# First ten MLP steps in plain float32, weights converted a whole tile at a time: a retention layer and two MLPs on one core

## The chip, the core and the metric

One core of a Trainium2 chip runs the whole program. Its engines are TensorE (PE in the profile; PEld is its weight load), VectorE (DVE), ScalarE (ACT), GpSimd (POOL) and SyncE (SP), whose queue issues most transfers (DMA). The metric is the device time of one execution in microseconds; lower is better.

## What is computed

```python
# retention: q, k, v of shape (4, 8, 768, 64)
gamma = 1.0 - 2.0 ** (-5.0 - np.arange(H, dtype=np.float32))
for t in range(S):
    state = gamma * state + np.einsum('bhd,bhe->bhde', k[:, :, t], v[:, :, t])
    y[:, :, t] = scale * np.einsum('bhd,bhde->bhe', q[:, :, t], state)
x = y.transpose(0, 2, 1, 3).reshape(3072, 512)
# MLP 1: 512 -> 2048 -> 512
h = x @ moe_w_in;  x = np.maximum(0.01 * h, h) @ moe_w_out
# MLP 2
h = np.maximum(x @ moe2_w_in, 0.0);  out = (h * h) @ moe2_w_out
```

The weights arrive as 64-bit floats, so the kernel turns them into 32-bit ones.

## The kernel before

**Retention** is done in chunks of 256 positions. A *unit* is one chunk of one batch element (12 units), a *pair* is two heads of one unit (48 pairs). A pair needs scaled q and v on VectorE (`qs`, `vs`, L121 and L122), scores on TensorE (`sc`, L168 and L169 in the first four units, L176 later), a masked product on VectorE (`pm`, L186), a value product on TensorE (`y`, L228 or L208), an outer product for the state (`sp` or `first_acc`, L243) and a copy into `xs`. The buffers of scores, outer products and MLP products come from one pool of three (`ps_h`).

**The MLPs** run in steps. A step takes one tile `j` of 128 of the 2048 hidden columns, for 512 tokens: an input group on TensorE (`emit_in`, product `h`), the activation on ScalarE and VectorE (`activate`, `g`), and an output group (`emit_out`) that adds into `acc`. In reduced precision each operand is split into a rounded value and the rest (`wih`/`wil`, `woh`/`wol`, `xh`/`xl`, `gh`/`gl`: a cast on ScalarE and a subtraction on VectorE), and three products stand for one: 12 of 512 columns in each group. The first `HS` = 5 steps are different: only unit 0 (256 tokens) is ready, and they run in plain float32, four products a group and no splits (L390, L437). Steps 5 to 15 take 512 tokens, steps 16 to 20 the other 256 of the first five tiles; after these 21 steps come blocks of 16, six blocks in each layer. Step `HS` writes its output in two cuts of 256 columns (`widens`).

**Weights.** Tile `j` of a layer is 1 MB in two halves (input and output weights). `load_half` brings one half into a staging buffer (`sg`), `convert` turns it into float32 (`w`): two ScalarE operations on the high and low words (L317, L318), then on VectorE a shift (L319), a merge of the sign (L320) and an add (L323). In the first layer two of three tiles stage in slots that later hold activations and the third in `stage_p`; in the second layer three half-tile buffers take turns.

**Order.** The code is written in step order, but a scheduler sets, when the program is built, the order in which each engine and queue gets its instructions; conversions are pulled ahead of steps where it finds room. On the chip each engine keeps that order, and an instruction that waits holds all behind it.

Of the kernel before, what the change touches and what calls it, by code (L numbers as in the profile page):

```python
# [9 lines left out]
F32 = mybir.dt.float32  # L10
# [19 lines left out]
LEAK = 0.01  # L30
WHOLE = 4
HS = 5
LEAD = 6
AHEAD = 2
AHEAD2 = 4
# [7 lines left out]
def retention_then_two_mlps(  # L43
# [11 lines left out]
    nc = tc.nc  # L55
    const = ctx.enter_context(tc.tile_pool(name="const", bufs=1))
    big_p = ctx.enter_context(tc.tile_pool(name="big", bufs=1))
    stage_p = ctx.enter_context(tc.tile_pool(name="stage", bufs=2))
    wsp_p = ctx.enter_context(tc.tile_pool(name="wsp", bufs=2))
    g_p = ctx.enter_context(tc.tile_pool(name="g", bufs=2))  # L60
    a_p = ctx.enter_context(tc.tile_pool(name="a", bufs=2))
# [11 lines left out]
    def slot(n, shape, dt, name):  # L73
        return big_p.tile(shape, dt, tag=f"x{n}", name=name)
# [87 lines left out]
    def scores(hu):  # L162
        u, p, h = hu
        if u < WHOLE:
            qs, k, vs = prep[u, p]
            a = slice(64 * h, 64 * h + 64)
            sc = ps_h.tile([P, 512], F32, tag="h", name="sc")
            nc.tensor.matmul(out=sc[:, 128:256], lhsT=k[a, P:2 * P], rhs=qs[a, P:2 * P], start=True, stop=True)  # L168
            nc.tensor.matmul(out=sc[:, 256:512], lhsT=k[a, 0:P], rhs=qs[a], start=True, stop=True)  # L169
        else:  # L170
            q2, kh, kl, v2, vs, w2 = prep[u, p]
            sc = ps_h.tile([P, 512], F32, tag="h", name="sc")
            for sb in (1, 0):
                o, c = (P, P) if sb else (C, 0)
                for n, kk in enumerate((kh, kl)):
                    nc.tensor.matmul(  # L176
                        out=sc[:, o:o + C - c], lhsT=kk[:, h * C + sb * P:h * C + (sb + 1) * P], rhs=q2[h][:, c:C],
                        start=n == 0, stop=n == 1,
                    )
        sc_ps[hu] = sc  # L180

# [91 lines left out]


    wraw, stage = {}, {}
    halves = [(lay, j, half) for lay in range(2) for j in range(NJ) for half in range(2)]
    n_loaded, n_conv = [0], [0]
    early_stage = [None]

    def load_half():  # L280
        m = n_loaded[0]
        if m < len(halves):
            lay, j, half = halves[m]
            if lay == 0 and half == 0 and j % 3 < 2:
                early_stage[0] = slot(4 + j % 3, [P, 2, DM], U64, "sg")
            if lay == 0 and j % 3 < 2:
                t = early_stage[0][:, half]
            elif lay == 0:
                t = stage_p.tile([P, DM], U64, tag="sg", name="sg")
            elif m % 3 == 2:  # L290
                t = a_p.tile([P, DM], U64, tag="r", name="sg", bufs=1)
            else:
                t = stage_p.tile([P, DM], U64, tag="sg", name="sg")
            stage[m] = t
            nc.sync.dma_start(out=t, in_=w[lay, j, half])
            n_loaded[0] += 1

    def convert():

        m = n_conv[0]
        n_conv[0] += 1
        lay, j, half = halves[m]
        if half == 0:  # L310
            wraw[lay, j] = rawslot((lay * NJ + j) % NRAW, [P, 2 * DM], F32, "w")
        r = wraw[lay, j][:, half * DM:(half + 1) * DM]
        src = stage.pop(m).bitcast(U32)
        word = src.rearrange("p (n t) -> p n t", t=2)
        lo, hi = word[:, :, 0], word[:, :, 1]
        ru = r.bitcast(U32)
        nc.scalar.activation(out=r, in_=hi.bitcast(F32), func=AF.Copy, scale=2.0 ** -112)  # L317
        nc.scalar.activation(out=lo, in_=lo, func=AF.Copy, scale=2.0 ** -29)  # L318
        nc.vector.tensor_scalar(out=ru, in0=ru, scalar1=3, scalar2=None, op0=ALU.logical_shift_left)  # L319
        nc.vector.scalar_tensor_tensor(  # L320
            out=ru, in0=hi, scalar=0x80000000, in1=ru, op0=ALU.bitwise_and, op1=ALU.bitwise_or,
        )
        nc.vector.tensor_tensor(out=ru, in0=ru, in1=lo, op=ALU.add)  # L323
        if n_loaded[0] < 2 * NJ or lay == 1:
            load_half()
        if m == 0:
            load_half()

    def converted_to(n):
        while n_conv[0] < min(n, len(halves)):  # L330
            convert()


# [18 lines left out]

    def split_w(i, half):
        n, j = steps[i][:2]
        if i < HS:
            (win, wout)[half][i] = wraw[lbs[n][0], j][:, half * DM:(half + 1) * DM]
            return
        src = wraw[lbs[n][0], j][:, half * DM:(half + 1) * DM]
        tag = ("wi", "wo")[half]
        hi = wsp_p.tile([P, DM], F32R, tag=tag + "h", name=tag + "h")  # L360
        lo = wsp_p.tile([P, DM], F32R, tag=tag + "l", name=tag + "l")
        nc.scalar.copy(hi, src)  # L362
        nc.vector.tensor_tensor(out=lo, in0=src, in1=hi.bitcast(F32), op=ALU.subtract)  # L363
        (win, wout)[half][i] = (hi, lo)
# [18 lines left out]
    def emit_in(i):  # L383
        n, j, c0, c1 = steps[i]
        hp = ps_h.tile([P, T], F32, tag="h", name="h")
        h_ps[i] = hp
        if i < HS:
            w, x = win.pop(i), xslot[0]
            for kb in range(KB):
                nc.tensor.matmul(  # L390
                    out=hp[:, :c1 - c0], lhsT=w[:, kb * P:(kb + 1) * P], rhs=x[:, kb, c0:c1],
                    start=kb == 0, stop=kb == KB - 1,
                )
            return
        x = xhl[n]
        wh, wl = win.pop(i)
        for kb in range(KB):
            xh, xl = x[kb]
            for k, (a, b) in enumerate(((wh, xh), (wl, xh), (wh, xl))):
                nc.tensor.matmul(  # L400
                    out=hp[:, :c1 - c0], lhsT=a[:, kb * P:(kb + 1) * P], rhs=b[:, c0:c1],
                    start=kb == 0 and k == 0, stop=kb == KB - 1 and k == 2,
                )

    def activate(i):
        n, j, c0, c1 = steps[i]
        lay, m = lbs[n][0], c1 - c0
        hp = h_ps.pop(i)
        g = g_p.tile([P, T], F32, tag="g", name="g", bufs=1)
        if i >= HS:  # L410
            gh = g_p.tile([P, T], F32R, tag="gh", name="gh")
            gl = g_p.tile([P, T], F32R, tag="gl", name="gl")
        if lay == 0:
            nc.scalar.activation(out=g[:, :m], in_=hp[:, :m], func=AF.Copy, scale=LEAK)  # L414
            nc.vector.tensor_tensor(out=g[:, :m], in0=g[:, :m], in1=hp[:, :m], op=ALU.max)  # L415
        else:
            nc.scalar.activation(out=g[:, :m], in_=hp[:, :m], func=AF.Relu)  # L417
            nc.vector.scalar_tensor_tensor(  # L418
                out=g[:, :m], in0=hp[:, :m], scalar=0.0, in1=g[:, :m], op0=ALU.max, op1=ALU.mult
            )  # L420
        if i < HS:
            gs[i] = g
            return
        nc.scalar.copy(gh[:, :m], g[:, :m])  # L424
        nc.vector.tensor_tensor(out=gl[:, :m], in0=g[:, :m], in1=gh[:, :m].bitcast(F32), op=ALU.subtract)  # L425
        gs[i] = (gh, gl)

    def emit_out(i):
# [2 lines left out]
        if i == first_step[n]:  # L431
            acc[n] = ps_acc.tile([P, 4, T], F32, tag="acc", name="acc")
        ac = acc[n]
        if i < HS:
            g, w = gs.pop(i), wout.pop(i)
            for m in range(4):
                nc.tensor.matmul(  # L437
                    out=ac[:, m, c0:c1], lhsT=w[:, m * P:(m + 1) * P], rhs=g[:, :c1 - c0], start=i == 0, stop=False
                )
            return  # L440
        gh, gl = gs.pop(i)
        wh, wl = wout.pop(i)

        start, stop = i == first_step[n], i == last_step[n]
        cols = [(c0, c1)]
        if i in widens:
            cols = [(c, c + C) for c in range(c0, c1, C)]
        passes = ((wh, gh), (wl, gh), (wh, gl))
        if stop:
            mm = [(k, m) for m in range(4) for k in range(3)]  # L450
# [53 lines left out]

    def need_x(i):
        n, j, c0, c1 = steps[i]
        if i < HS:
            return
        miss = [c for c in range(c0 // C, c1 // C) if (n, c) not in done_x]
        if miss:  # L510
# [20 lines left out]
    nc.scalar.dma_start(out=mk, in_=mask)  # L531
    loads_to(1)
    nc.scalar.dma_start(out=qt[:, 1:4], in_=qtab[:, 1:4])
    loads_to(4)
    for _ in range(5):
        load_half()
    first_acc = ps_acc.tile([P, 4, T], F32, tag="acc", name="first_acc")
    for k in range(NP):
        preps_to(k + 1)
# [5 lines left out]
    split_w(0, 0)  # L545
    emit_in(0)
    activate(0)
    converted_to(2)
    split_w(0, 1)
    converted_to(3)  # L550
    split_w(1, 0)
    converted_to(6)

    for i in range(N):
        n, j, c0, c1 = steps[i]
# [24 lines left out]
            preps_to(ups.index(head_at[i + 1][-1][:2]) + 1)  # L580
            loads_to(n_prep[0] + 1)
        if i < NJ:
            converted_to(min(2 * (i + 1 + AHEAD) + 1, 2 * NJ))
        if i == conv2 - AHEAD2 - 1:
            for _ in range(3):
                load_half()
        elif i >= conv2 - AHEAD2:
            j = i - conv2
            due = 2 * (i + 1 + AHEAD - first_step[NB]) + 1
            converted_to(2 * NJ + max(min(j + AHEAD2, 2 * max(j, 0) + 2), due))  # L590


_OUT = ((NT, DM), "float32")
# [58 lines left out]
```

## Time and profile before

| what | value |
|---|---|
| time, median of 3 runs | 1216.43 us (1216.36 to 1216.61) |
| profiled execution: its time | 1216.53 us |
| profiled execution: span of the trace | 1214.5 us |
| TensorE busy | 1187.4 us (98%) |
| VectorE busy | 863.0 us (71%) |
| ScalarE busy | 691.8 us (57%) |
| moved by DMA | 68.81 MB |

The span runs from the first instruction to the last; about 2 us of the time lie around it. Busy time of TensorE counts matmuls whose ends are modelled, and neighbours overlap, so the distance between the starts of two matmuls says more than their durations. The shares are means over stages that differ: the early stage (retention's first pairs, the first layer's conversions), the long middle, the second layer's conversions around 590 to 700 us, and the second layer.

### The profile page before, as it was taken

Reading aid. Unit: us, or ns where it says so; the run is one execution under the profiler, and the core shown is the slowest. Engines: PE = TensorE matmul, PEld = TensorE weight load, DVE = VectorE, ACT = ScalarE, POOL = GpSimd, SP = SyncE. Lnnn points to the kernel's source line nnn. Section 1 sums busy time; section 2 is a strip of 40 time slices with the busy share of each in tenths; the row PEclk is TensorE's granted clock in tenths of the full one; section 3 lists DMA queues with packets and bytes.
Section 4 is the critical chain, followed back from the end, with each engine's and each line's share of the span. In section 5 each row is a group of like instructions: output and inputs, shape, how many; then the busy total and the mean of one; then the engine's idle time right before and its main releaser. Section 6 shows DMA issues by size and latency. Waiting matters only on the chain.

```text
span 1214.5 us, 15223 instructions
## 1 busy us (share of the span) xinstructions
PE 1187.4 (98%) x5660; PEld 977.7 (81%) x5660; DVE 863.0 (71%) x1621; ACT 691.8 (57%) x1382; POOL 0.2 (0%) x4
## 2 busy tenths in 40 slices
PE   6889999999999999999999999999999999999998
PEld 4667788888888888888888788888888888888886
DVE  6996598889888888978799945644645545545553
ACT  5674476667666766766677644444444444444443
POOL 0000000000000000000000000000000000000000
PEclk9899999999999999999999999999999999999999
DMA  9662111111111111111145300000000000000000
GB/s 343 238 232 86 45 51 45 44 44 49 61 40 36 40 48 35 35 53 48 40 157 179 99 1 1 35 1 1 35 1 1 36 1 1 35 1 1 35 1 35
DMA packets 22825, 68.81 MB, mean 57 GB/s; under 512 B 2784, under 2 KB 5088, under 8 KB 22752
## 3 DMA queue, kind: packets, MB, share of 16 engines
q1 hardware_dynamic: 22032, 67.12, 16.3%
q8 instruction: 44, 0.72, 0.2%
q10 hardware_dynamic: 720, 0.73, 0.2%
q14 instruction: 29, 0.24, 0.1%
HBM read 61.55 MB, written 6.29 MB: 56 GB/s over the span
## 4 chain that ended last, share of the span: by engine, by line
PE 83%; DVE 10%; DMA 4%; ACT 2%; issue 1%; ACTq 0%; SPq 0%; DVEq 0%
PE acc L460 38%; PE h L400 37%; DMA sg<-w 3%; PE sc L176 2%; PE y L208 2%; DVE w L320 2%; DVE w L323 2%; DVE wil L363 1%; PE sp L243 1%; DVE w L319 1%; PE y L202 1%; DVE pm L186 1%; DVE g L415 1%; DVE wol L363 1%; DVE gl L425 1%
## 5 line engine op out<-in xcount | busy, mean ns | idle before, releaser
L400 PE MATMUL h<-xh,wih 128*128 128x512 f32 (+1 forms) x768 | 300.4, 391 | 2.8 <-DVE g L415 1.2
L400 PE MATMUL h<-xh,wil 128*128 128x512 f32 (+1 forms) x768 | 298.2, 388 | 0.0
L400 PE MATMUL h<-xl,wih 128*128 128x512 f32 (+1 forms) x768 | 297.9, 388 | 0.1
L363 DVE TENSOR_TENSOR wol<-w,woh 128x512 fp32r<-128x512 f32 x192 | 132.4, 690 | 135.5 <-ACT woh L362 134.1
L362 ACT CAST woh<-w 128x512 fp32r<-128x512 f32 x192 | 119.3, 621 | 174.7 <-PE acc L460 173.5
L400 PEld LDWEIGHTS h<-xh,wih 128*128 128x128 f32 x768 | 144.5, 188 | 33.4 <-DVE g L415 2.5
L400 PEld LDWEIGHTS h<-xl,wih 128*128 128x128 f32 x768 | 144.3, 188 | 30.3 <-issue 1.0
L400 PEld LDWEIGHTS h<-xh,wil 128*128 128x128 f32 x768 | 144.5, 188 | 28.7 <-DVE wil L363 1.3
L425 DVE TENSOR_TENSOR gl<-g,gh 128x512 fp32r<-128x512 f32 (+1 forms) x192 | 130.7, 680 | 26.4 <-PE acc L460 12.7
L424 ACT CAST gh<-g 128x512 fp32r<-128x512 f32 (+1 forms) x192 | 118.1, 615 | 47.2 <-DVE g L418 26.8
L363 DVE TENSOR_TENSOR wil<-w,wih 128x512 fp32r<-128x512 f32 x192 | 131.4, 684 | 5.8 <-ACT wih L362 5.3
L362 ACT CAST wih<-w 128x512 fp32r<-128x512 f32 x192 | 117.8, 614 | 11.0 <-PE h L400 10.5
L460 PE MATMUL acc<-gh,woh 128*128 128x512 f32 (+1 forms) x388 | 109.5, 395 | 2.1 <-ACT gh L424 2.1
L418 DVE SCALAR_TENSOR_TENSOR g<-h,g 128x512 f32<-128x512 f32 x96 | 66.2, 690 | 59.2 <-ACT g L417 58.3
L460 PE MATMUL acc<-gh,wol 128*128 128x512 f32 (+1 forms) x388 | 106.2, 386 | 0.0
L460 PE MATMUL acc<-gl,woh 128*128 128x512 f32 (+1 forms) x388 | 105.9, 384 | 0.0
L460 PE MATMUL acc<-wol,gh 128*128 128x512 f32 x384 | 105.5, 389 | 0.0
L460 PE MATMUL acc<-woh,gh 128*128 128x512 f32 x384 | 105.5, 389 | 0.0
L460 PE MATMUL acc<-woh,gl 128*128 128x512 f32 x384 | 105.5, 389 | 0.0
L417 ACT ACTIVATE g<-h 128x512 f32<-128x512 f32 x96 | 57.3, 597 | 72.8 <-PE h L400 67.9
L414 ACT ACTIVATE g<-h 128x512 f32<-128x512 f32 (+1 forms) x101 | 57.9, 573 | 52.5 <-PE h L400 43.5
L460 PEld LDWEIGHTS acc<-woh,gl 128*128 128x128 f32 x384 | 72.1, 188 | 15.0
(81 smaller groups left out, 1490.0 us busy)
## 6 DMA issues: line engine op xcount, KB each, us to landing
sg<-w SPq DMA_DIRECT2D x64, 512.0 KB, 4.0
r<-attn SPq DMA_DIRECT2D x32, 512.0 KB, 3.5
re<-first SPq DMA_DIRECT2D x12, 512.0 KB, 5.7
out<-os SPq DMA_DIRECT2D x24, 256.0 KB, 2.0
kn<-attn SPq DMA_DIRECT2D x16, 128.0 KB, 2.1
r<-first SPq DMA_DIRECT2D x3, 512.0 KB, 5.7
r<-first SPq DMA_DIRECT2D x2, 256.0 KB, 3.1
qt<-qtab ACTq DMA_DIRECT2D x1, 384.0 KB, 7.8
```

Of the source, the lines that this page charges most:

```text
L176: nc.tensor.matmul(out=sc[:, o:o + C - c], lhsT=kk[:, h * C + sb * P:h * C + (sb + 1) * P], rhs=q2[h][:, c:C], start=n == 0, stop=n == 1,)
L208: nc.tensor.matmul(out=y[:, c:C], lhsT=v2[:, sb, h].rearrange("p a e -> p (a e)"), rhs=t[:, n, o:o + C - c], start=start, stop=n == 1 and ...
L320: nc.vector.scalar_tensor_tensor(out=ru, in0=hi, scalar=0x80000000, in1=ru, op0=ALU.bitwise_and, op1=ALU.bitwise_or,)
L362: nc.scalar.copy(hi, src)
L363: nc.vector.tensor_tensor(out=lo, in0=src, in1=hi.bitcast(F32), op=ALU.subtract)
L400: nc.tensor.matmul(out=hp[:, :c1 - c0], lhsT=a[:, kb * P:(kb + 1) * P], rhs=b[:, c0:c1], start=kb == 0 and k == 0, stop=kb == KB - 1 and k ...
L414: nc.scalar.activation(out=g[:, :m], in_=hp[:, :m], func=AF.Copy, scale=LEAK)
L417: nc.scalar.activation(out=g[:, :m], in_=hp[:, :m], func=AF.Relu)
L418: nc.vector.scalar_tensor_tensor(out=g[:, :m], in0=hp[:, :m], scalar=0.0, in1=g[:, :m], op0=ALU.max, op1=ALU.mult)
L424: nc.scalar.copy(gh[:, :m], g[:, :m])
L425: nc.vector.tensor_tensor(out=gl[:, :m], in0=g[:, :m], in1=gh[:, :m].bitcast(F32), op=ALU.subtract)
L460: nc.tensor.matmul(out=o, lhsT=lhsT, rhs=rhs, start=start and k == 0, stop=stop and k == 2)
```

## The change

- Steps 0 to 9 (`WS` = 10) run in plain float32 instead of 0 to 4; steps 5 to 9 do so for all 512 tokens (the units 0 and 1). Their weights, inputs and `g` are not split; the split of x is first needed for step 10.
- `load_tile` and `convert` handle a whole tile: two transfers into one buffer, then each operation once over 1024 columns (2048 half-words in the add). `stage_p` holds one such tile, and in the second layer it is the only staging buffer.
- At the start the loads of the first pairs and of the first three weight tiles alternate.
- Later scores (L176) run wide, narrow, wide, narrow in one accumulation group instead of narrow, narrow, wide, wide in two.
- The due times of conversions are given in tiles.

```diff
+WS = 10
-    stage_p = ctx.enter_context(tc.tile_pool(name="stage", bufs=2))
+    stage_p = ctx.enter_context(tc.tile_pool(name="stage", bufs=1))
...
-            for sb in (1, 0):
-                o, c = (P, P) if sb else (C, 0)
-                for n, kk in enumerate((kh, kl)):
+
+            for n, kk in enumerate((kh, kl)):
+                for sb in range(2):
+                    o, c = (P, P) if sb else (C, 0)
                     nc.tensor.matmul(
                         out=sc[:, o:o + C - c], lhsT=kk[:, h * C + sb * P:h * C + (sb + 1) * P], rhs=q2[h][:, c:C],
-                        start=n == 0, stop=n == 1,
+                        start=n == 0 and sb == 0, stop=n == 1 and sb == 1,
                     )
...
+    def load_tile():
         m = n_loaded[0]
...
+        if m < len(tiles):
+            lay, j = tiles[m]
             if lay == 0 and j % 3 < 2:
...
+                t = slot(4 + j % 3, [P, 2, DM], U64, "sg")
             else:
-                t = stage_p.tile([P, DM], U64, tag="sg", name="sg")
+                t = stage_p.tile([P, 2, DM], U64, tag="sg", name="sg")
             stage[m] = t
-            nc.sync.dma_start(out=t, in_=w[lay, j, half])
+            for half in range(2):
+                nc.sync.dma_start(out=t[:, half], in_=w[lay, j, half])
             n_loaded[0] += 1
...
+        lay, j = tiles[m]
+        r = wraw[lay, j] = rawslot((lay * NJ + j) % NRAW, [P, 2 * DM], F32, "w")
+        src = stage.pop(m).rearrange("p h n -> p (h n)").bitcast(U32)
...
-        if i < HS:
+        if i < WS:
             (win, wout)[half][i] = wraw[lbs[n][0], j][:, half * DM:(half + 1) * DM]
             return
...
+        if i < WS:
+            g, w = gs.pop(i), wout.pop(i)
+            for m in range(4):
+                for s0, s1 in cols:
+                    nc.tensor.matmul(
+                        out=ac[:, m, s0:s1], lhsT=w[:, m * P:(m + 1) * P], rhs=g[:, s0 - c0:s1 - c0],
+                        start=i == 0, stop=False,
+                    )
+            return
...
+    loads_to(2)
+    load_tile()
+    loads_to(3)
+    load_tile()
     loads_to(4)
-    for _ in range(5):
-        load_half()
+    load_tile()
```

VectorE's order moves most. Before, around pair 9's masked products (`pm_665`, `pm_667`; `w_1011` to `w_1148` are tiles in conversion, `wol` a weight split):

```order
L320 SCALAR_TENSOR_TENSOR w_1089<-sg_928,w_1089 128x512
L122 TENSOR_TENSOR vs_700<-re_623,vt_86 128x256
L323 ISA w_1011<-sg_779,w_1011 128x1024
L323 ISA w_1089<-sg_854,w_1089 128x1024
L363 TENSOR_TENSOR wol_681<-w_537,woh_680 128x512
L319 TENSOR_SCALAR w_1148<-w_1148 128x512
L186 TENSOR_TENSOR pm_665<-sc_659,mk_87 128x384
L323 ISA w_1089<-sg_928,w_1089 128x1024
L186 TENSOR_TENSOR pm_667<-sc_662,mk_87 128x384
```

Of the change, on VectorE, around step 5's maximum (`g_446`; `pm_482` and `pm_484` belong to pair 8, `w_717` and `w_793` are the 13th and 14th tile in conversion):

```order
L313 TENSOR_SCALAR w_717<-w_717 128x1024
L314 SCALAR_TENSOR_TENSOR w_717<-sg_566,w_717 128x1024
L313 TENSOR_SCALAR w_793<-w_793 128x1024
L188 TENSOR_TENSOR pm_482<-sc_476,mk_87 128x384
L317 ISA w_717<-sg_566,w_717 128x2048
L355 TENSOR_TENSOR wil_704<-w_633,wih_703 128x512
L314 SCALAR_TENSOR_TENSOR w_793<-sg_593,w_793 128x1024
L355 TENSOR_TENSOR wol_768<-w_633,woh_767 128x512
L407 TENSOR_TENSOR g_446<-g_446,h_441 128x512
L188 TENSOR_TENSOR pm_484<-sc_479,mk_87 128x384
```

Conversions now stand ahead of step 5's maximum that stood behind it; the two cuts of each are one row.

In the second layer's conversions, on VectorE of the change (`w_6348`, `w_6437` are tiles 3 and 4 of that layer, `sg_6354` the one staging buffer in its next turn):

```order
L317 ISA w_6348<-sg_6265,w_6348 128x2048
L355 TENSOR_TENSOR wol_6289<-w_342,woh_6288 128x512
L417 TENSOR_TENSOR gl_6283<-g_6281,gh_6282 128x512
L355 TENSOR_TENSOR wol_6329<-w_390,woh_6328 128x512
L407 TENSOR_TENSOR g_6321<-g_6321,h_6308 128x512
L355 TENSOR_TENSOR wil_6382<-w_459,wih_6381 128x512
L417 TENSOR_TENSOR gl_6323<-g_6321,gh_6322 128x512
L313 TENSOR_SCALAR w_6437<-w_6437 128x1024
L314 SCALAR_TENSOR_TENSOR w_6437<-sg_6354,w_6437 128x1024
L355 TENSOR_TENSOR wol_6378<-w_432,woh_6377 128x512
L317 ISA w_6437<-sg_6354,w_6437 128x2048
```

Between the last operation on one tile, which frees the buffer, and the first on the next stand the six operations of one and a half steps, and one more stands inside the turn. Over the whole layer 14 such turns now lie in 26 steps; before, 15 tiles lay in some 20 steps.

## Rows read from the trace of the kernel before

**Rows 1.** The page, busy time by engine: busy us, share, instructions.

```profile
PE 1187.4 (98%) x5660; PEld 977.7 (81%) x5660; DVE 863.0 (71%) x1621; ACT 691.8 (57%) x1382; POOL 0.2 (0%) x4
```

**Rows 2.** Windows: stretch, its length, busy us (instructions) by engine, clock, DMA share, GB/s.

```profile
15.00:98.00 83.00, 71.09 (x350) 51.18 (x350) 79.40 (x162) 58.31 (x115) 0.00 (x0) 0.92 0.70 251
...
674.00:700.00 26.00, 24.14 (x103) 18.59 (x102) 24.77 (x44) 17.18 (x31) 0.00 (x0) 1.00 0.26 82
```

**Rows 3.** Waits of VectorE, 0 to 98 us: us in total, times, longest.

```profile
DVE vs L122 <- DMA r<-first: 4.7, 1, 4.7
DVE vs L122 <- PE y L228: 2.9, 2, 1.9
DVE w L156 <- ACT w L153: 2.1, 1, 2.1
DVE w L319 <- ACT w L317: 1.7, 3, 0.7
DVE vs L122 <- DMA re<-first: 1.7, 1, 1.7
DVE w L323 <- ACT sg L318: 0.5, 1, 0.5
```

**Rows 4.** Timeline of VectorE: start us, duration us, line, operation.

```profile
25.62 0.42 DVE L122 TENSOR_TENSOR vs<-r,vt 128x256 f32<-128x256 f32 x1
25.95 0.68 DVE L323 CUSTOM_DVE_ANT_0 w<-sg,w 128x1024 uint16<-128x1024 uint16 x1
26.56 0.55 DVE L186 TENSOR_TENSOR pm<-sc,mk 128x384 f32<-128x384 f32 x1
27.02 0.42 DVE L319 TENSOR_SCALAR w<-w 128x512 uint32<-128x512 uint32 x1
27.36 0.55 DVE L186 TENSOR_TENSOR pm<-sc,mk 128x384 f32<-128x384 f32 x1
```

**Rows 5.** The chain of waits, 86 to 113 us: start us, us, what.

```profile
89.34 0.56 DVE pm L186
...
90.04 0.87 PE y L228 x8
```

**Rows 6.** Timeline of TensorE, plain float32 groups and one pair.

```profile
43.25 0.50 PE L168 MATMUL sc<-qs,re 64*128 64x128 f32 x4
...
44.11 1.99 PE L437 MATMUL acc<-g,w 128*128 128x256 f32 x8
45.94 0.61 PE L243 MATMUL sp<-vs,re 128*128 128x128 f32 x4
46.96 0.87 PE L228 MATMUL y<-pm,vs 128*64 128x256 f32 x8 [0.41 <-DVE pm L186]
47.76 1.99 PE L390 MATMUL h<-xs,w 128*128 128x256 f32 x8
```

**Rows 7.** Windows again, around TensorE's last early idle time.

```profile
77.00:81.00 4.00, 3.89 (x19) 3.70 (x20) 4.00 (x10) 3.94 (x9) 0.00 (x0) 0.61 0.88 351
```

**Rows 8.** The chain of waits, one group of twelve reduced products.

```profile
727.92 2.72 PE h L400 x12
```

**Rows 9.** Timeline of TensorE, value products and scores in the middle.

```profile
303.34 0.28 PE L202 MATMUL y<-q,w 128*128 128x256 f32 x1
...
304.04 0.63 PE L460 MATMUL acc<-gl,woh 128*128 128x512 f32 x2
...
307.48 0.22 PE L176 MATMUL sc<-q,kh 128*128 128x128 f32 x1
...
307.94 0.34 PE L208 MATMUL y<-ph,v 128*128 128x256 f32 x2
```

**Rows 10.** Line L295 from 51.8 to 52.5 us: two half-tile loads.

```profile
L295 SPq DMA_DIRECT2D sg<-w x2: 328/377/426, 51.9 to 52.3; - x2
...
DMA to landing us min/median/max: 3.5/3.9/4.4
```

**Rows 11.** Groups by line and shape, whole span: busy us, mean ns.

```profile
L317 ACT ACTIVATE w<-sg 128x512 f32<-128x512 f32 x64 | 42.8, 674 | 30.8 <-DMA sg<-w 29.2 <-DVE wol L363 1.3
```

More of the change, by code (lines that the diff above doesn't have):

```diff
@@ L275, in retention_then_two_mlps @@
     wraw, stage = {}, {}
-    halves = [(lay, j, half) for lay in range(2) for j in range(NJ) for half in range(2)]
+    tiles = [(lay, j) for lay in range(2) for j in range(NJ)]
     n_loaded, n_conv = [0], [0]
-    early_stage = [None]
-    def load_half():
+    def load_tile():
         m = n_loaded[0]
[L282 to L285, printed above, removed]
+        if m < len(tiles):
+            lay, j = tiles[m]
             if lay == 0 and j % 3 < 2:
-                t = early_stage[0][:, half]
-            elif lay == 0:
-                t = stage_p.tile([P, DM], U64, tag="sg", name="sg")
-            elif m % 3 == 2:
-                t = a_p.tile([P, DM], U64, tag="r", name="sg", bufs=1)
+                t = slot(4 + j % 3, [P, 2, DM], U64, "sg")
             else:
-                t = stage_p.tile([P, DM], U64, tag="sg", name="sg")
+                t = stage_p.tile([P, 2, DM], U64, tag="sg", name="sg")
             stage[m] = t
-            nc.sync.dma_start(out=t, in_=w[lay, j, half])
+            for half in range(2):
+                nc.sync.dma_start(out=t[:, half], in_=w[lay, j, half])
             n_loaded[0] += 1
@@ L308, in convert @@
         n_conv[0] += 1
[L309 to L313, printed above, removed]
+        lay, j = tiles[m]
+        r = wraw[lay, j] = rawslot((lay * NJ + j) % NRAW, [P, 2 * DM], F32, "w")
+        src = stage.pop(m).rearrange("p h n -> p (h n)").bitcast(U32)
         word = src.rearrange("p (n t) -> p n t", t=2)
@@ L323, in convert @@
         nc.vector.tensor_tensor(out=ru, in0=ru, in1=lo, op=ALU.add)
-        if n_loaded[0] < 2 * NJ or lay == 1:
-            load_half()
-        if m == 0:
-            load_half()
+        if n_loaded[0] < NJ or lay == 1:
+            load_tile()
     def converted_to(n):
-        while n_conv[0] < min(n, len(halves)):
+        while n_conv[0] < min(n, len(tiles)):
             convert()
@@ L386, in emit_in @@
         h_ps[i] = hp
-        if i < HS:
+        if i < WS:
             w, x = win.pop(i), xslot[0]
@@ L409, in activate @@
         g = g_p.tile([P, T], F32, tag="g", name="g", bufs=1)
-        if i >= HS:
+        if i >= WS:
             gh = g_p.tile([P, T], F32R, tag="gh", name="gh")
@@ L420, in activate @@
             )
-        if i < HS:
+        if i < WS:
             gs[i] = g
@@ L433, in emit_out @@
         ac = acc[n]
-        if i < HS:
+        cols = [(c0, c1)]
+        if i in widens:
+            cols = [(c, c + C) for c in range(c0, c1, C)]
+        if i < WS:
             g, w = gs.pop(i), wout.pop(i)
             for m in range(4):
-                nc.tensor.matmul(
-                    out=ac[:, m, c0:c1], lhsT=w[:, m * P:(m + 1) * P], rhs=g[:, :c1 - c0], start=i == 0, stop=False
-                )
+                for s0, s1 in cols:
[3 more added lines that the diff above has]
+                    )
             return
@@ L444, in emit_out @@
         start, stop = i == first_step[n], i == last_step[n]
-        cols = [(c0, c1)]
-        if i in widens:
-            cols = [(c, c + C) for c in range(c0, c1, C)]
         passes = ((wh, gh), (wl, gh), (wh, gl))
@@ L506, in need_x @@
         n, j, c0, c1 = steps[i]
-        if i < HS:
+        if i < WS:
             return
@@ L533, in retention_then_two_mlps @@
     nc.scalar.dma_start(out=qt[:, 1:4], in_=qtab[:, 1:4])
+    loads_to(2)
+    load_tile()
+    loads_to(3)
+    load_tile()
     loads_to(4)
-    for _ in range(5):
-        load_half()
+    load_tile()
     first_acc = ps_acc.tile([P, 4, T], F32, tag="acc", name="first_acc")
@@ L547, in retention_then_two_mlps @@
     activate(0)
+    split_w(0, 1)
     converted_to(2)
-    split_w(0, 1)
+    split_w(1, 0)
     converted_to(3)
-    split_w(1, 0)
-    converted_to(6)
     for i in range(N):
@@ L582, in retention_then_two_mlps @@
         if i < NJ:
-            converted_to(min(2 * (i + 1 + AHEAD) + 1, 2 * NJ))
+            converted_to(min(i + 2 + AHEAD, NJ))
         if i == conv2 - AHEAD2 - 1:
-            for _ in range(3):
-                load_half()
+            load_tile()
         elif i >= conv2 - AHEAD2:
             j = i - conv2
-            due = 2 * (i + 1 + AHEAD - first_step[NB]) + 1
-            converted_to(2 * NJ + max(min(j + AHEAD2, 2 * max(j, 0) + 2), due))
+            due = i + 2 + AHEAD - first_step[NB]
+            converted_to(NJ + max(min((j + AHEAD2) // 2, max(j, 0) + 1), due))
 _OUT = ((NT, DM), "float32")
```

## The prediction

> **What bounds the kernel now.** I read the page first: TensorE is busy 98% of the span [rows 1]. A busy matmul can still be one that waits, so the next view is the table of windows [rows 2]. Between 15 and 98 us TensorE is busy 71.09 of 83 us while VectorE is busy 79.40: the early stage is VectorE's. From 674 to 700 us TensorE is again short of its stretch, 24.14 of 26.00, with VectorE at 24.77. Everywhere else TensorE works back to back, and there only TensorE's own work counts. So three things decide: when TensorE stops waiting in the early stage, how much TensorE work the new float32 steps add, and whether the stall near 674 us stays.
>
> The chain of waits tells when the early stage ends: VectorE's masked product of pair 9 ends at 89.34 + 0.56 = 89.90, TensorE's value product of that pair starts at 90.04 [rows 5], and from there the chain is on TensorE. I count to this place.
>
> **Prices on VectorE.** In the timeline the starts of back-to-back operations give the price [rows 4]: 512 columns 0.60 (25.95 to 26.56), 256 columns 0.34 (25.62 to 25.95), a 384-column masked product 0.47, a 512-column shift 0.34. From 256 to 512 columns the price grows by 0.27, so about 0.07 is fixed; a 1024-column operation is taken at 0.60 + 0.53 = 1.14, a 1024-column shift at 0.60. [...] A whole tile is thus 2.87 instead of 3.08.
>
> **VectorE, before.** Its order up to pair 9's second masked product holds 31 shifts, 30 merges and 30 adds of half tiles (10.4 + 36.1), 20 masked products (9.4), 21 scalings of q or v (7.1), 5 narrow and 2 wide maxima (2.9), 9 splits of weights and g (5.4), the split of x (3.1), 0.5 for two small ones: 74.9 us. It ends at 89.9, so 15.0 us were lost. The waits [rows 3] name 13.6 of them: 4.7, 2.1 and 1.7 at the start, 2.9 for a value product to free a buffer, 2.2 for ScalarE's half of a conversion.
>
> **VectorE, after.** The new order lets TensorE wait at another place: step 5's maximum g_446 stands behind fourteen started tile conversions. Ahead of it, with it: 14 shifts (8.4), 14 merges (15.9), 13 adds (14.8), 17 masked products (8.0), 19 scalings (6.4), 5 narrow maxima and this one (2.3), 4 weight splits (2.4), the split of x (3.1), 0.5: 61.8 us. The start (8.5) is the same work and the same loads. The first conversion then waits some 0.7 for its data, and the 1.4 that [rows 3] leave unnamed I keep. The remaining 5.1 us of waits may vanish or return; I take 1.5. That is 12.1 lost, bounds 10.6 and 15.0, so g_446 ends at 73.9 (72.4 to 76.8). The loads are no later: the same bytes are queued, pair 2 and pair 3 land behind weight tiles but, at the spacing of the old queue, before VectorE reaches them. A tile must now land whole; its cover is the two tiles ahead of it in the three staging buffers, and without that the bound of 15.0 applies.
>
> **TensorE, prices.** Four float32 products of 256 columns, which the trace lists as eight, run from 44.11 to 45.94: 1.83 [rows 6]. Four of 512 columns are twice the columns: 3.66 at most, 3.43 if the 0.1 at the start of each group is paid once and the rest runs at 0.215 per listed half; I take 3.5. The twelve reduced products that they replace take 2.72 [rows 8]. So each of the ten groups of steps 5 to 9 costs 0.8 more, 7.6 in all (6.5 to 9; step 5's second half is cut in 256 columns in both kernels and costs about the same).
>
> **TensorE, the sum.** What TensorE had finished when it started pair 9's value product, it still has partly before it at g_446: the output products of steps 5 and 6 and the input products of step 7 (3.5 each), pair 8's outer and value products (0.6 + 0.8) and pair 9's scores and outer product (0.9 + 0.6) [rows 6]: 13.4. Just ahead of g_446 TensorE idles for some 4 of 6 us, since its score buffers are all held until that maximum. [...] So that place is reached at 73.9 + 13.4 + 1.7 = 89.0 instead of 90.0, a gain of 1.0. Behind it stand five groups of 3.5 instead of 2.72, 3.9 more. First stage: +2.9 us. From step 10 on TensorE has the same work; the casts and subtractions of ten weight halves and five g that fall away lay beside it.
>
> **Scores.** The same four products in another order. Today narrow, narrow, wide, wide take 0.46 (307.48 to 307.94); where wide and narrow already alternate in the value products, six take 0.70 (303.34 to 304.04), 0.117 each, or 0.47 for four [rows 9]. Both run at the pace of the weight loads. Price: 0, bounds 64 x 0.01 more and 64 x 0.11 less, if the narrow ones' 0.06 each were all that counted.
>
> **The second layer's weights.** Conversion there used three half-tile buffers; now one whole-tile buffer, so a tile's load starts only when the tile before is finished. One turn: two halves issued 0.4 apart, the second landing 4.4 later [rows 10], 4.8; ScalarE's operation, 0.67 for 512 columns [rows 11], some 1.1 for 1024; VectorE 2.87; hand-overs 0.3: 9.1. The new order puts one or two other operations of 0.60 inside nearly every turn: 10.1 on average, 142 us for 14 turns. They are spread over 26 steps; a step is two groups of 2.72 [rows 8], 141 us. It just fits, and VectorE's density falls: 2.87 per two steps instead of per 1.3. So I expect most of the old stall of 1.9 to go (a busy end is modelled, so the true stall is nearer 3): -2.0, bounds -3 and +4.
>
> The sum is +2.9 - 2.0 = +0.9. The profiled execution took 1216.5, as did the runs (1216.36 to 1216.61): 1217.4.
>
> **The rivals.**
> 1. *Forecast: no change that can be told*, 1217.4. A measurement here can tell about 0.2%, 2.4 us, so this is 1214.0 to 1218.9. Chance 0.42.
> 2. *Faster: VectorE keeps none of the avoidable waits and the clock stays up.* g_446 at 72.4, no 1.7: the first stage is 72.4 + 13.4 - 90.0 + 3.9 = -0.3, and with the second layer's stall wholly gone (-3) the time is 1213.2; at 3.43 per float32 group 1212.6. For it: the masked products and loads ahead are all on time in my count. Against: in the trace of before every such hand-over cost something. Chance 0.16.
> 3. *Faster: an operation costs its mean duration, not the distance to the next.* Then merging two saves more: 0.69 against 0.42 for 256 columns makes 0.15 fixed instead of 0.07, 41 operations x 0.08 = 3.3 us earlier, 1214.1, at the edge of what can be told. The starts in [rows 4] speak against it. Chance 0.05. [...]
> 4. *Faster: the score order hides weight loads*, 64 x 0.11 = 7 us at most, 1210. The alternating value products in [rows 9] speak against it. Chance 0.04.
> 5. *Slower: the single buffer of the second layer sets the pace.* If a turn is 0.5 longer (ScalarE busy when a tile lands, a later landing), 14 turns are 7 us late; some 2.5 lie in TensorE's lead of half a step, 4.5 stall it: 2.9 + 4.5 - 3 = +4.4, 1220.9. It decides from a turn of about 10.5 us on. For it: with three buffers ScalarE already waits for these loads today; against: VectorE has more room. Chance 0.18. [...]
> 6. *Slower: VectorE loses 15.0 us again*, since whole tiles arrive later than halves. g_446 at 76.8: +5.8 - 2.0 = +3.8, 1220.3. Chance 0.15. That the change does not do what it says is not a case: steps 5 to 9 are float32 in the new order.
>
> **How the numbers follow.** The time is that of case 1. Faster 2 to 4: 0.25; slower 5 and 6: 0.33. From 1211.5 (case 2 at the low price, with a third of case 3) to 1224 (5 and 6 together, 1217.4 + 3.5 + 2.9) leaves out the score case, and late loads together with float32 groups of 3.66.
>
> **What would show it.** Right: TensorE's last early wait ends near 74 us, on step 5's maximum; then the granted clock is low for one stretch; four wide float32 products take 3.4 to 3.7; TensorE hardly waits near 674 us; turns of the weight buffer in the second layer last about 10 us. Wrong: waits of VectorE for ScalarE's conversions in the first 75 us beyond 3 us, or a row of TensorE waits of 0.5 us or more spread from 620 to 760 us.

## The result and the profile after

| kernel | median | runs |
|---|---|---|
| before | 1216.52 us | 1216.36 to 1216.61, 4 runs |
| changed | 1226.38 us | 1224.9 to 1227.99, 4 runs |

The changed kernel is slower: ratio 1.0087, 95% interval 1.0074 to 1.0100. The profiled execution took 1225.2 us, its span is 1223.4, 8.9 more than before. The page, busy time by engine, against [rows 1]:

```profile
PE 1192.7 (97%) x5616; PEld 970.8 (79%) x5616; DVE 847.3 (69%) x1510; ACT 676.2 (55%) x1303; POOL 0.2 (0%) x4
```

VectorE has 16 us less to do, TensorE 5 more, and the time is up by 9.9. To see where, I take the same matmul in both traces, counted back from the last one (behind step 10 the two programs have the same matmuls), and compare its start:

| stretch | forecast | measured |
|---|---|---|
| to about 135 us | +2.9 | +7.6 |
| from there to 590 us | 0 | +0.4 |
| 590 to 800 us (second layer's weights) | -2.0 | +0.95 |
| rest | 0 | 0 |

**The early stage.** Windows of the changed kernel (columns as in [rows 2]):

```profile
15.00:98.00 83.00, 70.03 (x306) 44.35 (x305) 72.17 (x104) 49.17 (x71) 0.00 (x0) 0.94 0.73 261
...
76.00:80.00 4.00, 1.97 (x7) 1.79 (x8) 4.00 (x7) 1.36 (x2) 0.00 (x0) 0.50 0.78 262
80.00:84.00 4.00, 4.00 (x17) 3.10 (x15) 4.00 (x5) 2.68 (x4) 0.00 (x0) 0.77 0.39 131
84.00:98.00 14.00, 13.35 (x53) 6.50 (x53) 7.59 (x11) 4.62 (x8) 0.00 (x0) 1.00 0.47 162
```

VectorE's relief is there (72.17 of 83 us instead of 79.40), but look where: in the last 14 us it works 7.59. Until 84 us it is as full as ever, and TensorE waits for it. The timeline of TensorE shows the two last waits (in brackets: idle time ahead, and who ended it):

```profile
74.28 0.59 PE L170 MATMUL sc<-qs,r 64*128 64x256 f32 x2
78.03 1.23 PE L245 MATMUL sp<-vs,r 128*128 128x128 f32 x4 [3.15 <-DVE g L407]
79.04 5.00 PE L434 MATMUL acc<-g,w 128*128 128x256 f32 x16
...
89.27 3.70 PE L434 MATMUL acc<-g,w 128*128 128x512 f32 x8
92.81 0.61 PE L245 MATMUL sp<-vs,re 128*128 128x128 f32 x4
94.06 0.87 PE L230 MATMUL y<-pm,vs 128*64 128x256 f32 x8 [0.65 <-DVE pm L188]
```

The place is the one forecast, step 5's maximum, but at 78 us and not at 73.9, and pair 9's mask is late once more. VectorE's timelines have that maximum, before and changed:

```profile
74.19 0.68 DVE L415 TENSOR_TENSOR g<-g,h 128x512 f32<-128x512 f32 x1
```

```profile
77.29 0.68 DVE L407 TENSOR_TENSOR g<-g,h 128x512 f32<-128x512 f32 x1
```

Step 5's output products (listed as 16 of 256 columns) then take 5.00, at a granted clock of 0.50 and 0.77. Waits of VectorE from 0 to 98 us, against [rows 3]:

```profile
DVE w L313 <- ACT w L311: 6.7, 5, 3.1
DVE vs L123 <- DMA r<-first: 4.8, 1, 4.8
DVE vs L123 <- DMA re<-first: 2.4, 1, 2.4
DVE w L157 <- ACT w L154: 2.1, 1, 2.1
...
```

The wait for ScalarE's half of a conversion grew from 2.2 to 6.7: 3.6 of it by 75 us, which is more than the 3 that the prediction named as a sign of being wrong, and 3.1 at 89.9 us, ahead of pair 9's mask. In the longest of the early ones ScalarE itself waits for a tile: one load, 6.88 us, in the chain of waits, and VectorE behind it in its timeline:

```profile
40.78 6.88 DMA sg<-w
47.74 1.15 ACT w L311
```

```profile
46.09 1.22 DVE L314 SCALAR_TENSOR_TENSOR w<-sg,w 128x1024 uint32<-128x1024 uint32 x1
48.91 0.69 DVE L313 TENSOR_SCALAR w<-w 128x1024 uint32<-128x1024 uint32 x1 [1.60 <-ACT w L311]
```

**Behind it** the chain is on TensorE. One float32 group there:

```profile
102.00 3.43 PE acc L434 x8
```

**The second layer.** Loads into the one staging buffer, 600 to 760 us, and two of TensorE's waits (its timeline):

```profile
L291 SPq DMA_DIRECT2D sg<-w x28: 327/378/436, 608.8 to 745.1; - x28
...
DMA to landing us min/median/max: 3.4/4.1/4.9
```

```profile
670.31 0.97 PE L454 MATMUL acc<-gh,woh 128*128 128x512 f32 x3 [0.78 <-ACT gh L416]
...
704.87 0.50 PE L392 MATMUL h<-xh,wil 128*128 128x512 f32 x1 [0.87 <-DVE wil L355]
```

28 half loads, two a turn: from the first turn's start to the last one's, 13 turns, (745.1 - 0.4 - 608.8) / 13 = 10.45 us each, against 10.1 forecast. 10.1 is also what 26 steps of 5.44 us leave for each of 14 turns, so 13 turns come 4.6 us late. TensorE waits at four places spread from 669 to 755 us (0.78, 0.36, 0.87 and 0.55), no longer in one stretch: the prediction's other sign of being wrong.

### The profile page after: what moved, and what is told of

It is laid out like the page before. It is cut to its first block, busy times and chain, and to the rows that moved or that the text cites. A ratio compares the mean times of both kernels' runs of the same rounds, so it can differ in the third digit from the quotient of the medians.

```text
span 1223.4 us, 14940 instructions
## 1 busy us (share of the span) xinstructions
PE 1192.7 (97%) x5616; PEld 970.8 (79%) x5616; DVE 847.3 (69%) x1510; ACT 676.2 (55%) x1303; POOL 0.2 (0%) x4
## 3 DMA queue, kind: packets, MB, share of 16 engines
q1 hardware_dynamic: 22032, 67.12, 16.1%
## 4 chain that ended last, share of the span: by engine, by line
PE 78%; DVE 9%; DMA 8%; ACT 3%; issue 2%; SPq 0%; ACTq 0%; DVEq 0%
PE acc L454 35%; PE h L392 35%; DMA sg<-w 7%; PE sc L178 2%; PE y L210 2%; DVE w L317 2%; DVE w L314 2%; ACT w L311 2%; DVE w L313 1%; PE acc L434 1%; PE sp L245 1%; PE y L204 1%; DVE pm L188 1%; DVE g L407 1%; DVE wol L355 1%
## 5 line engine op out<-in xcount | busy, mean ns | idle before, releaser
L392 PE MATMUL h<-xh,wih 128*128 128x512 f32 (+1 forms) x748 | 292.1, 390 | 0.7 <-DVE g L407 0.7
L392 PE MATMUL h<-xh,wil 128*128 128x512 f32 (+1 forms) x748 | 290.3, 388 | 1.2 <-DVE wil L355 1.2
L392 PE MATMUL h<-xl,wih 128*128 128x512 f32 (+1 forms) x748 | 290.5, 388 | 0.1
L392 PEld LDWEIGHTS h<-xh,wil 128*128 128x128 f32 x748 | 140.5, 188 | 30.7 <-DVE wil L355 3.4
L392 PEld LDWEIGHTS h<-xl,wih 128*128 128x128 f32 x748 | 140.5, 188 | 28.7 <-issue 0.5
L392 PEld LDWEIGHTS h<-xh,wih 128*128 128x128 f32 x748 | 140.6, 188 | 28.3 <-DVE g L407 0.8
L354 ACT CAST wih<-w 128x512 fp32r<-128x512 f32 x187 | 114.8, 614 | 11.2 <-PE h L392 10.7
L454 PE MATMUL acc<-gh,woh 128*128 128x512 f32 (+1 forms) x364 | 103.4, 397 | 0.8 <-ACT gh L416 0.8
L454 PE MATMUL acc<-gh,wol 128*128 128x512 f32 (+1 forms) x364 | 100.8, 386 | 0.0
L454 PE MATMUL acc<-gl,woh 128*128 128x512 f32 (+1 forms) x364 | 99.1, 384 | 0.1
L454 PEld LDWEIGHTS acc<-woh,gh 128*128 128x128 f32 x384 | 72.0, 188 | 15.9 <-ACT gh L416 1.0
```

Of the source, the lines that this page charges most:

```text
L392: nc.tensor.matmul(out=hp[:, :c1 - c0], lhsT=a[:, kb * P:(kb + 1) * P], rhs=b[:, c0:c1], start=kb == 0 and k == 0, stop=kb == KB - 1 and k ...
L454: nc.tensor.matmul(out=o, lhsT=lhsT, rhs=rhs, start=start and k == 0, stop=stop and k == 2)
```

## The experiments

Three theories of the early loss. **A:** the ten float32 steps; their price is not covered. **B:** whole tiles land late in single buffers. **C:** one conversion that stands too early. A fourth, **O**, came from the first group: what counts is how much work the order puts ahead of step 5's maximum. The kernel before ran beside each group (medians 1216.12, 1216.61 and 1216.07); there single runs of one kernel lie 3 to 5 us apart, so medians are compared.

**e1, five steps.**

```diff
-WS = 10
+WS = 5
```

> The change with five plain float32 steps instead of ten; whole tiles, alternating loads, score order and the one staging buffer stay. Theory A (the ten steps: their extra products are TensorE time behind pair 9, and the VectorE time that they free is filled with conversions pulled ahead): the 3.5 us behind pair 9 go; VectorE has 70.3 us of work up to pair 9's second masked product and loses 15 to 19.6, so pair 9's value product starts at 85.5 to 90; with the second layer's 0.9 more the time is 1213 to 1217.5. Theory B (whole tiles that land late make VectorE wait; the steps matter little): it loses as much as now at as late a place, pair 9's value product near 94, and the time is 1220 to 1223.

Measured: 1219.02 us, ratio to before 1.0019 (1.0006 to 1.0031). The early stage is 0.8 ahead of before, so the loss there has gone with the steps, as A has it. Pair 9's second masked product ends at 87.0 (93.9 in the change), also as A has it; the value product starts only at 92.6, outside A's 85.5 to 90, since TensorE's order here has other work ahead of it. The time lies between the two ranges, 1.5 above A's, since the second layer costs 3.4, though its code is that of the changed kernel. Its worst place, TensorE's timeline and a window behind it:

```profile
698.08 0.80 PE L392 MATMUL h<-xh,wil 128*128 128x512 f32 x1 [1.86 <-DVE wil L355]
698.67 0.63 PE L392 MATMUL h<-xl,wih 128*128 128x512 f32 x1
699.10 0.63 PE L392 MATMUL h<-xh,wih 128*128 128x512 f32 x1
```

```profile
695.00:698.00 3.00, 0.94 (x3) 0.20 (x2) 3.00 (x6) 1.69 (x5) 0.00 (x0) 0.99 0.19 40
698.00:701.00 3.00, 2.92 (x7) 2.34 (x8) 1.82 (x4) 0.56 (x2) 0.00 (x0) 0.50 0.79 310
```

A late weight idles TensorE for 1.86 us, and then the matmuls start 0.43 apart (698.67 to 699.10) instead of 0.23 (694.82 to 695.05), at a granted clock of 0.50.

**e2, ten steps alone**, on the kernel before (the other `HS` tests that the change turns into `WS` too):

```diff
+WS = 10
...
-        if i < HS:
+        if i < WS:
             w, x = win.pop(i), xslot[0]
```

> The kernel before with ten plain float32 steps and nothing else of the change: half tiles, three staging buffers, old loads and old score order. Its VectorE order has the same 74.9 us of work up to pair 9's second masked product as before. Theory A: pair 9 near 90, then five groups of 0.7 more, 3.5; 1219.5 to 1222. Theory B: the steps cost little, because the whole tiles are what is slow: 1215.5 to 1218.5.

Measured: 1222.14 us, 1.0047 (1.0035 to 1.0059), early stage +6.5, second layer +0.1. The steps alone bring most of the loss, with half tiles and the old loads: A. It is just above A's range: step 5's maximum ended at 76.6, later than before (74.9), and pair 9's value product started at 93.0, not near 90.

**e3, sixteen tile slots**, on the change; the 17th slot lets the second layer's first tile be converted at 89.9 to 93.4 us, ahead of pair 9's mask.

```diff
-    NRAW = NJ + 1
+    NRAW = NJ
```

> The change with 16 float32 tile slots instead of 17. The order differs in one thing only: the conversion of the second layer's first tile (the 17th), which stands ahead of pair 9's second masked product and waits 3.1 us for its load, moves to the last block of the first layer. Theory C (that early conversion is the loss): VectorE is 6.0 us earlier at pair 9, the time falls by 4 to 6, 1219 to 1222. Theory A or B (TensorE comes late from step 5's maximum anyway and waits only 0.6 us for pair 9): it falls by 0.5 to 1.6, 1223.5 to 1226, less up to 1 us that the later conversion may cost in the second layer.

Measured: 1225.45 us, 1.0068 (1.0055 to 1.0081), early stage +6.8 instead of +7.6, in the range of A or B. Pair 9's value product comes at 93.24 instead of 94.06, without the wait of 0.65; but the maximum also ended 0.4 earlier, so C was worth at most 0.8.

**e4, half tiles where there is one buffer**, on the change (`h0`, `h1` are the halves that an item has; in the second layer two buffers `sg` and one `r`, as before):

```diff
+    for lay in range(2):
+        for j in range(NJ):
+            items += [(lay, j, 0, 2)] if lay == 0 and j % 3 < 2 else [(lay, j, 0, 1), (lay, j, 1, 2)]
...
```

> The change, but with half tiles wherever the change has a single staging buffer: every third tile of the first layer in two half buffers, and the second layer in the three half buffers of before; the other first-layer tiles stay whole, ten steps, alternating loads and score order stay. Theory B: the early waits for late whole tiles fall by 2 to 4 us and the second layer is as before, together 1219.5 to 1222.5. Theory A: only the second layer's 0.9 comes back: 1223.5 to 1225.5.

Measured: 1221.15 us, 1.0037 (1.0025 to 1.0049). The early stage is at +2.7 and the second layer at -0.4. B's number, but the maximum also has less work ahead of it in this order: 58.6 us instead of 61.7. So two readings were left, and the next group separates them.

**e5, the change again**, unaltered.

> The changed kernel once more, unaltered, for a second profile and as the base of this group. If the single staging buffer of the second layer makes turns that differ from execution to execution, the stall between 660 and 760 us differs from the 4.0 us of the first profile by half a us or more (the kernel with five steps and the same buffer had 6.5), while the early stage repeats within 0.8; if the loss in the second layer is fixed by the order, it repeats within 0.3. Time 1225 to 1228.

Measured: 1227.83 us, 1.0092 (1.0079 to 1.0105). The maximum ends at 78.9, the early stage is +8.7, the second layer +1.55: the early stage differs by 1.1 from the first profile (expected within 0.8), the second layer by 0.6, so neither is fixed by the order, and both losses are there again.

**e6, the change with the loads of before at the start.**

```diff
-    loads_to(2)
-    load_tile()
-    loads_to(3)
-    load_tile()
     loads_to(4)
-    load_tile()
+    for _ in range(3):
+        load_tile()
```

> The change with the loads of before at the start: four pairs, then three weight tiles. In the order that follows VectorE has 56.5 us of work up to step 5's maximum with 12 tiles converted ahead, instead of 61.8 with 13, and 68.4 instead of 74.2 up to pair 9's second masked product. Theory O (what stands ahead of step 5's maximum decides): the maximum ends at 72 to 74 instead of 78.0 and the time falls by 3 to 5, 1221 to 1223.5. Theory B (late tiles decide: now the first one lands later still): VectorE loses what it has less to do, the maximum stays at 76.5 to 79, 1225 to 1228.

Measured: 1224.73 us, 1.0074 (1.0061 to 1.0087), 3.1 less than e5. VectorE's timeline has step 5's maximum 7.3 us earlier:

```profile
69.96 0.68 DVE L407 TENSOR_TENSOR g<-g,h 128x512 f32<-128x512 f32 x1
```

The maximum is earlier than even O had it (72 to 74), and B's bet (late first tile, no gain) falls; the fall of the time is in O's 3 to 5, though the time itself lies between the two ranges. The profiled execution was the quickest of six (1220.8 to 1227.7), with an early stage of +0.75.

**e7, the alternating loads alone**, on the kernel before:

```diff
-    loads_to(4)
-    for _ in range(5):
-        load_half()
+    loads_to(2)
+    load_half()
+    load_half()
+    loads_to(3)
+    load_half()
+    load_half()
+    loads_to(4)
+    load_half()
```

> The kernel before with the alternating loads alone (half tiles: two after the second pair, two after the third, one after the fourth). VectorE's work up to pair 9's second masked product is 73.7 instead of 74.9. Theory O: 1 us earlier, 1215 to 1216.5. Theory B: pair 2 and pair 3 land behind weights and the start loses 1 to 2: 1216.5 to 1218.5.

Measured: 1216.03 us, 0.9998 (0.9989 to 1.0007): no difference, in O's range. The work ahead of the maximum (60.9 against 59.9) and its end (75.4 against 74.9) hardly moved. The loads are not slow by themselves; in the change they made the order worse.

**e8, what is left**: e4 with `WS = 5`.

> Five plain float32 steps, whole-tile conversion only where a whole tile has a slot of its own, half tiles in the third slot and in the second layer (three half buffers), alternating loads, new score order. If the ten steps and the single whole-tile buffer are the two losses, what is left of the change is its gain: VectorE 58.5 us of work and 14 to 15 lost up to step 5's maximum, 72.5 to 73.5; early stage 1 to 2.5 ahead of before, the second layer as before: 1213.5 to 1215.5, against 1216.1 to 1216.5 of before. If the whole-tile conversions or the alternation are themselves a loss: 1217 to 1220.

Measured: 1215.66 us, 0.9995 (0.9987 to 1.0004): 6.0 below e4 against the kernel before, not told apart from before. Early stage -2.0, as expected; the maximum (73.9) and the time are just above their ranges, and the second layer gave back 1.2.

**e9, e6 again**, unaltered.

> The ten-step change with the loads of before once more, for a second profile: its first group of runs lay between 1220.8 and 1227.7, and the profiled one was the quickest. If the early stage repeats (step 5's maximum at 70 to 72, early stage 0 to 2 behind before) the spread arises later, in the middle or in the second layer: 1220.5 to 1225. If waits of VectorE for loads in the early stage come and go, the maximum lies anywhere from 70.6 to 78: 1221 to 1228.

Measured: 1224.24 us, 1.0063 (1.0048 to 1.0077). The maximum ends at 72.6, the early stage is +3.9 in an execution of 1224.0. So waits of VectorE come and go by some 2 to 3 us between executions of this kernel, and part of e6's gain was luck of its profile; the medians agree (1224.73, 1224.24).

**e10, whole tiles alone**: the change with `WS = 5`, the loads of before (as in e6) and the score order of before.

> The whole-tile conversions alone with their single staging buffer: five plain float32 steps, loads and score order of before. VectorE has 56.0 us of work up to step 5's maximum with 11 tiles ahead, and 67.4 up to pair 9's second masked product with 13 (before: 59.9 and 74.9 with 12 and 15). Theory O (what stands ahead decides): with 14 to 15 lost the maximum ends at 70 to 71 and pair 9 some 5 us earlier than before; second layer 1 to 3.4 worse: 1212.5 to 1216. Theory B (the single buffer is late wherever it is used): pair 9 no earlier, 1217 to 1220.

Measured: 1217.94 us, 1.0015 (1.0005 to 1.0025). Early stage -2.1, second layer +4.7. The time is in B's range, but not for B's reason: the early stage is ahead, as O has it (by less: the maximum ends at 72.3, and pair 9's value product starts at 89.3, 0.8 earlier and not 5, though its mask is 6.1 earlier), and the second layer takes back more than O's bound of 3.4.

**e11, e8 with the loads of before.**

> As the five-step kernel with whole tiles only where a slot holds one and half tiles elsewhere, but with the loads of before; new score order. VectorE: 56.7 us of work up to step 5's maximum with 11 tiles ahead (58.5 with 12 in the alternating one), 72.5 up to pair 9's second masked product. Theory O: 1.5 to 2 us ahead of the alternating one, 1212.5 to 1214.5. If the place of the loads makes no difference: 1215 to 1216.5.

Measured: 1213.97 us, 0.9979 (0.9970 to 0.9988): in O's range, and 2.1 us faster than the kernel before. VectorE's timeline at the maximum, and a window of the second layer's conversions:

```profile
69.95 0.68 DVE L403 TENSOR_TENSOR g<-g,h 128x512 f32<-128x512 f32 x1
```

```profile
680.00:700.00 20.00, 19.29 (x83) 15.04 (x82) 16.88 (x29) 11.48 (x21) 0.00 (x0) 1.00 0.17 53
```

The early stage is 3.3 ahead of before; in the second layer, where TensorE is short by 0.71 of these 20 us, it loses 1.25 of that again.

**e12, e4 with the loads of before.**

> The ten-step kernel with half tiles where the change has a single buffer, now with the loads of before. VectorE's work up to step 5's maximum is 58.5 us with 12 tiles ahead, the same as in its alternating form (58.6, where the maximum ended at 72.8). Theory O (the work in front decides, not the landing of the loads): the same time, 1220 to 1222.5. If the alternating loads cost by themselves: 3 us less, 1217 to 1219.

Measured: 1220.45 us, 1.0036 (1.0021 to 1.0051); e4 was 1.0037. The same work ahead (58.5 and 58.6), the same end of the maximum (72.6 and 72.8), the same time: O, and the place of the loads costs nothing by itself.

All profiles together. Work: VectorE's operations up to step 5's maximum, counted from the order with the prices of the prediction; lost: the maximum's end less that; early and second layer as in the first table; time: median less that of the kernel before beside it.

| kernel | steps | work | maximum ends | lost | early | second layer | time |
|---|---|---|---|---|---|---|---|
| before | 5 | 59.9 | 74.9 | 15.0 | 0 | 0 | 0 |
| change | 10 | 61.7 | 78.0 | 16.3 | +7.6 | +0.95 | +9.9 |
| e5 (change) | 10 | 61.7 | 78.9 | 17.2 | +8.7 | +1.55 | +11.2 |
| e3 | 10 | 61.7 | 77.5 | 15.8 | +6.8 | +0.45 | +9.3 |
| e2 | 10 | 60.9 | 76.6 | 15.7 | +6.5 | +0.1 | +6.0 |
| e6 | 10 | 56.5 | 70.6 | 14.1 | +0.75 | +0.95 | +8.1 |
| e9 (e6) | 10 | 56.5 | 72.6 | 16.1 | +3.9 | +1.4 | +8.2 |
| e4 | 10 | 58.6 | 72.8 | 14.2 | +2.7 | -0.4 | +5.0 |
| e12 | 10 | 58.5 | 72.6 | 14.1 | +1.9 | -0.3 | +4.4 |
| e7 | 5 | 60.9 | 75.4 | 14.5 | +0.4 | -1.1 | -0.6 |
| e1 | 5 | 58.8 | 74.8 | 16.0 | -0.8 | +3.35 | +2.9 |
| e10 | 5 | 56.0 | 72.3 | 16.3 | -2.1 | +4.7 | +1.9 |
| e8 | 5 | 58.5 | 73.9 | 15.4 | -2.0 | +1.2 | -1.0 |
| e11 | 5 | 56.7 | 70.6 | 13.9 | -3.3 | +1.25 | -2.1 |

## Why the prediction was wrong

1. **What bounds, and where: right.** VectorE holds TensorE, the last long wait is for step 5's maximum, and a stretch at a lower clock follows (0.50 in the window from 76 to 80 us). From 77.97 to pair 9 the way is 15.4 us (to the end of the outer product, about 93.4), forecast 13.4 + 1.7 = 15.1. The 1.7, which case 2 leaves out, is my estimate of what the lower clock costs on this way, and no run shows it as a term of its own; in its place the change showed a granted clock of 0.50 from 75.0 to 81.5 us and step 5's output products at 5.00 us instead of 3.43 to 3.7.
2. **The failed step: "The remaining 5.1 us of waits may vanish or return; I take 1.5."** 12.1 lost was the result, with 15.0 as the upper bound; the change lost 16.3. The start was about as counted (10.5 with the first conversion; 8.5 + 0.7 + 1.4 = 10.6 forecast); behind it 5.7 went instead of 1.5. Tiles that landed late cost 1.7 at 48.9 us and 0.7 at 72.7, so the cover of "the two tiles ahead of it" did not hold; products of TensorE and a cast cost 2.2, 0.8 of it at 18.7 us, where the tile had landed at 15.8 and ScalarE waited for an outer product first; some 1.1 went in small gaps between operations on the same tile. In 14 profiles the loss lies between 13.9 and 17.2, whatever was converted and loaded: taking work out of VectorE's order did not take the waits out of it. The kernels with the single whole-tile buffer lie at 14.1 to 17.2 (mean 16.0), the others at 13.9 to 15.7 (mean 14.7): 1.3 us that can be the buffer's, though two profiles of one kernel (e6, e9) differ by 2.0. Rival 6 had the place and the direction, but was sized too small (76.8 forecast there, 78.0 measured), and its reason, late whole tiles, is 2.4 of the 5.7.
3. **The work ahead was right (61.8 against 61.7), but I took it as given.** It is 1.8 more than before, although merged operations and unsplit weights had taken work out: the order put more conversions in their place. With the old loads it is 56.5. Each us of it is 1.0 to 1.7 us of the maximum (e6, e9, e4 and e12 against the change); a straight line through the 14 profiles gives 1.2.
4. **The price of a float32 group: right, 3.43 behind pair 9**, so 0.71 more than 2.72, and 7.1 for ten. (Two small slips in my prices change nothing: by its own rule the low price is 3.54 and not 3.43, and ten times 0.78 is 7.8 and not 7.6.) But only the five groups behind pair 9 (3.9; measured 3.5) were counted as loss, the others as time that an earlier VectorE hides. Five more steps cost 6.0 to 8.3 us of time in each of four settings: before to e2 6.0, e8 to e4 6.0, e11 to e12 6.5, e1 to e5 8.3 (7.0 to the first measurement of the change). That is about the full price: what the steps save on VectorE ahead of the maximum is filled with conversions (60.9 us of work in e2, 59.9 before), and the rest is saved behind it, where VectorE then works only 7.59 of 14 us.
5. **Pair 9's mask: missed.** It stood behind the second layer's first tile and its late load, 0.65 us beyond the maximum's chain; in e3, without that conversion, the wait is gone.
6. **Scores: about right.** Kernels with the new order lose 0.4 to 0.7 around 190 us, those without it (e2, e7, e10) none: in the change a wait of 0.66 for a maximum, ahead of 191.41 us. In the profile of the change 0.2 came back by 590 us.
7. **The second layer: wrong sign, rival 5 right.** Its turn is 10.45 us instead of 10.1; rival 5 decided "from a turn of about 10.5 us on", and gave the layer 4.5 - 3 = +1.5: measured +0.95 and +1.55. The traces speak for several buffers here: with three half buffers the layer stands at -0.4 to +0.1 with ten steps (e4, e12, e2) and at -1.1 to +1.25 with five (e7, e8, e11, before), with one whole buffer at +0.45 to +1.55 with ten steps and at +3.35 and +4.7 with five (e1, e10).
8. **Mean durations (case 3) fell:** a 1024-column merge is 1.14 from the next start (24.07 to 25.21 us), as priced. Two operations of 512 columns take 1.20 from start to start (0.60 each, [rows 4]) and one of 1024 takes 1.14: 0.06 saved, about the 0.07 of the price and not the 0.15 of case 3.

The misses add up: +4.1 (maximum), +0.3 (way), +0.65 (mask), -0.4 (behind), +0.4 (to 590 us), +2.95 (second layer) = 8.0, the 8.9 measured less the 0.9 forecast. Cases 5 and 6 came together, and their sum, 1223.8, was 1.4 short of the profiled 1225.2.

**Open.** In all ten-step profiles but the first, another 0.6 to 2.8 us go between 135 and 590 us, above all around 290 and 510; in the first profile of the change only 0.4, and e5, with the same order, has 1.7. The part at 290 can be followed to a transfer: in those seven profiles a load of attention data takes 4.1 to 4.7 us from issue to landing, in the first profile of the change 3.4; VectorE waits for it 1.4 to 1.9 us instead of 0.6, and TensorE then 0.4 to 1.1 us for `xs` instead of none. VectorE's timeline of the change and of e5, then TensorE's of e5:

```profile
289.57 0.43 DVE L122 TENSOR_TENSOR qs<-r,qt 128x256 f32<-128x256 f32 x1 [0.62 <-DMA r<-attn]
```

```profile
291.72 0.43 DVE L122 TENSOR_TENSOR qs<-r,qt 128x256 f32<-128x256 f32 x1 [1.67 <-DMA r<-attn]
```

```profile
297.04 0.36 PE L204 MATMUL y<-q,w 128*128 128x256 f32 x1 [0.84 <-DVE xs L274]
```

What makes that load slower was not tried, and neither was the part at 510. Not shown either is why the single buffer costs the second layer more with five steps than with ten. Nor was it tried to lower the 14 to 17 us that VectorE loses.

## What to carry to other kernels

An engine that is relieved is not early where it matters unless the relief stands ahead of its last deadline: count the work in its order up to the operation that the other engine waits for, not its total, and look at what the order puts into the gap. Waits in this dense stage were a level that stayed (14 to 17 us), not a sum of items that went away one by one; a forecast should keep them until a run shows them gone. And a buffer that is refilled only when it is empty has a turn of load, conversion and the neighbours' work: when that sum "just fits" the pace of its user, as here (10.1 forecast, 10.45 measured), count on a stall.

## What the runs showed of the hardware

- TensorE's clock also falls late in the program: in e1, after a stretch with 0.94 of 3 us busy, the next 3 us ran at 0.50, products 0.43 apart instead of 0.23. In the early stage of the change it fell in the wait before 78 us (TensorE idle from 74.87, 0.50 in the window from 76 to 80), and step 5's output products took 5.00, where eight listed ones of 512 columns, as many columns in all, take 3.43 to 3.7.
- In these two traces an operation of VectorE that works on what the one just before it wrote started later: in the change, a shift of 1024 columns followed by another tile's add is 0.60 from it, by its own tile's merge 0.71. In the kernel before, with 512 columns, a merge of another tile is 0.34 from the shift, that of the same tile 0.46. Timeline of the change:

```profile
31.98 0.68 DVE L313 TENSOR_SCALAR w<-w 128x1024 uint32<-128x1024 uint32 x1
32.69 1.23 DVE L314 SCALAR_TENSOR_TENSOR w<-sg,w 128x1024 uint32<-128x1024 uint32 x1
...
53.66 0.69 DVE L313 TENSOR_SCALAR w<-w 128x1024 uint32<-128x1024 uint32 x1
54.26 1.22 DVE L317 CUSTOM_DVE_ANT_0 w<-sg,w 128x2048 uint16<-128x2048 uint16 x1
```
